# Down-projection between the gate/up groups of the next tile, and single buffers for row sums

## The chip, the cores and the metric

The kernel runs on one NeuronCore of a Trainium2 chip. The metric is the device time of one execution in microseconds (us). TensorE (PE) multiplies, with its weight loads shown apart (PEld); ScalarE (ACT) computes the exponentials and tanh; VectorE (DVE) adds, scales and moves results out of PSUM; GpSimd (POOL) does a few small steps; SyncE (SP) issues every DMA from one in-order queue.

## The reference

A pre-norm transformer block on x of 2048 tokens by 1024, all in bfloat16. Attention has 32 query heads of 32 columns, and one key and one value head for all of them. The second half is a gated feed-forward network with 3584 inner columns:

```
xn = layernorm(x)
q, k, v = xn @ wq, xn @ wk, xn @ wv          # 32 heads of q, one of k and of v
p = softmax(q @ k.T * 32 ** -0.5)            # per head, 2048 x 2048
h = x + (p @ v, heads side by side) @ wo
hn = layernorm(h)
out = h + (sigmoid(hn @ w_gate) * (hn @ w_up)) @ w_down
```

## The kernel before, in words

Tokens are cut into 16 tiles of 128. A tile's attention is four **blocks** (`qi`, 64 in all), each of 8 heads by 128 queries. A block is 8 **visits**: 8 score matmuls (`emit_S`, the rows with `S_ps<-QTb,kT`), then two exponentials on ACT of 128x1024 each (line 567). That makes 512 visits and 1024 exponentials. DVE adds the 8 results of a block up in `acc` (line 544, 14 adds), from which one short run of PE (`acc,sel`, 32 matmuls) makes the row sums; 64 matmuls with `Vt` then give the unscaled output of the block. Both are one group, `PV`. The reciprocals of the row sums go through DRAM and come back spread over the partitions (`r_scratch`, `rb`, lines 626 and 627), and DVE scales with them (line 630, `OT`). `acc`, `r_sb`, `rb` and `oun` each have two buffers, used in turn by blocks.

After a tile's four blocks come its output projection (`OP`, 16 matmuls of 512 columns with `wo_sb`), the second layernorm, its transposes (`hT`, line 714), and the feed-forward network. Its first part is 14 **gate/up groups** (`GU`, rows with `hnT,ring`, 32 matmuls of 128 columns each): seven column groups of 512, each a gate group and an up group. Each group reads one **weight slab** of 1 MB (1024 x 512), loaded from DRAM in four DMAs (line 744) into one of four slots of `ring`. The groups run forward in even and backward in odd tiles, so the last four slabs of a tile are the first four of the next, and a tile loads ten. A slab's slot is reloaded as soon as its group has run. Gate goes through tanh (line 781) and both make `hact` (line 787). The second part is the down-projection (`D`, rows with `zone,hact`): 56 matmuls of 512 columns in two groups of 28, whose weights stay in SBUF.

The order on each engine is written out before the kernel is built, by a planner in the kernel itself (`Plan`). It walks along PE's time with assumed costs; whenever the scores of the next visit can run and ACT's backlog is under 1 us it puts a visit, else it goes on with the current group, else it picks the first group that is ready by the list `PRIO` (line 365). A gate/up group is only taken when the plan has its slab landed, by an assumed 330 bytes per ns for all DMAs, and slab loads are spaced for 310 (lines 40 and 41): a load that the spacing holds back gets a wait on an ACT instruction. The engines then run these orders strictly, with semaphores.

Of the kernel before, what the change touches and what calls it, by code (L numbers as in the profile page):

```python
# [12 lines left out]
P = 128  # L13
# [22 lines left out]
class Plan:  # L36
# [3 lines left out]
    DMA_RATE = 330.0  # L40
    PACE_RATE = 310.0
# [99 lines left out]
def bass_sequential_preLN__grouped_kv_mqa__glu_gated_glu__prompt_kernel(  # L141
# [30 lines left out]
    with ExitStack() as es:  # L172
# [10 lines left out]
        acc = SB("acc", [2, 2048])  # L183
# [11 lines left out]
        hnT = SB("hnT", [2, DT, P])  # L195
        hact = SB("hact", [NFT * P])
# [10 lines left out]
        r_dram = nc.dram_tensor("r_scratch", [2, 16, 64], F32, kind="Internal").ap()  # L207
# [17 lines left out]
        qst = hact[:, :].rearrange("p (a b) -> p a b", b=512)  # L225
# [8 lines left out]
        extra = [acc[:, 0, :], hnT[:, :, :, :].rearrange("p a b c -> p (a b c)"), acc[:, 1, :],  # L234
                 hn[:, :, :].rearrange("p a b -> p (a b)")]
        acc_slots = (extra[0], extra[2])
# [128 lines left out]
        PRIO = ["xT", "KV", "Q0", "PV", "OP", "hT", "D", "GU", "Q1", "Q"]  # L365
# [17 lines left out]
        def mk_xT(t):  # L383
# [6 lines left out]
            def after(b, last):  # L390
                src = F_ps[:, b, :].bitcast(BF16).rearrange("p (a b) -> p a b", a=DT)
                fa, fd = both(xnT[:, :, t * P:(t + 1) * P], src)
                xT_ev[t] = evac(fa, fd, 1024, [last], 2, 1.92, bias=300.0)
                if t + 2 < NT:
                    make_norm1(t + 2, [last])
                    if (t + 2) % 4 == 3:
                        load_slab((t + 2) // 4, [xnorm[k] for k in range(t - 1, t + 3)])
                queue_after_xT(t)
                return [xT_ev[t]]
# [147 lines left out]
        acc_rel = []  # L547

        def emit_S(v):
# [14 lines left out]
            for i in range(2):  # L564
# [6 lines left out]
                if qi >= 2 and kp >= 1:  # L571
                    if acc_busy[0]:
                        late_adds.append((qi, kp, i))
                    else:
                        make_add(qi, kp, i)
# [10 lines left out]
        oun_ev = {}  # L586

        def mk_PV(qi):
            c, qd = qi // 4, qi % 4
            raw = qi < 2  # L590
            srcs = [slot_of[(qi, kp)] for kp in range(NKP)] if raw else [acc[:, qi % 2, :]]

            def sum_done(o):
                sum_last[qi] = o

# [24 lines left out]
            def after(b, last):  # L620
                k = qi % 2
                rc = pl.op("dve", lambda: DVE.reciprocal(r_sb[:, k, :], F_ps[:, b, 256:320]),  # L622
                           [last] + rb_ld.get(qi - 2, []), prio=0, occ=64 * 8 / 0.96 + 20, lat=64 * 8 / 0.96 + 90 + SEM)
                oc = pl.op("dve", lambda: DVE.tensor_copy(out=oun[:, k, :], in_=F_ps[:, b, 0:256]),  # L624
                           [last, ot_ev.get(qi - 2)], prio=0, **t_dve(256))
                r1 = dma(lambda: SP.dma_start(r_dram[k], r_sb[0:P:8, k, :]), f"rd{k}", 4096, [rc], prio=0)
                rb_ld[qi] = [dma(lambda: SP.dma_start(
                    rb[:, k, :], bass.AP(r_dram.tensor, r_dram.offset + k * 1024, [[256, 4], [0, DH], [1, 256]])),
                    f"rb{k}", 131072, [r1, ot_ev.get(qi - 2)], prio=0)]
                ot_ev[qi] = pl.op("dve", lambda: DVE.tensor_tensor(  # L630
                    out=OT[:, 2 * qd:2 * qd + 2, :], in0=oun[:, k, :].rearrange("p (a b) -> p a b", a=2),
                    in1=rb[:, k, :].rearrange("p (a b) -> p a b", a=2), op=ALU.mult),
                    [oc, op_last.get(c - 1)] + rb_ld[qi], prio=0, occ=330, lat=420)
# [16 lines left out]
        def release(qi, kp, o):  # L650
# [6 lines left out]
            else:  # L657
                extra_rel.append(o)
                if any(s is a for a in acc_slots):
                    acc_rel.append(o)  # L660
                    acc_busy[0] -= 1
                    if acc_busy[0] == 0:
                        for k in late_adds:
                            make_add(*k)
# [22 lines left out]
        def mk_OP(t, dc):  # L687
# [19 lines left out]
            def gate():  # L707
                return t in xr_ld and xr_ld[t].end is not None
            return Group("OP", atoms, lambda: [ot_ev[4 * t + i] for i in range(4)] + [wo_ld], after, gate)

        def mk_hT(t):
# [5 lines left out]
            def after(b, last):  # L717
                hT_last[t] = last
                src = F_ps[:, b, :].bitcast(BF16).rearrange("p (a b) -> p a b", a=DT)
                hT_ev[t] = pl.op("dve", lambda: DVE.tensor_copy(out=hnT[:, t % 2, :, :], in_=src),  # L720
                                 [last, gu_last.get(t - 2)] + (extra_rel if t < 2 else []), prio=1, **t_dve(1024, 1.92))
                for i in range(NGR):
                    mk_GU(t, i)
# [3 lines left out]


        def group_of(t, i):
            return i if t % 2 == 0 else NGR - 1 - i  # L730

        slab_seq = [(t, i, w) for t in range(NT) for i in range(NGR) for w in range(2) if t == 0 or i >= 2]
        slab_n = [0]
        slab_at = {}

        def load_slab(sl, deps):
            if slab_n[0] >= len(slab_seq):
                return
# [9 lines left out]
            slab_at[(t, i, w)] = (sl, ops)  # L748
            if i >= NGR - 2:
                slab_at[(t + 1, NGR - 1 - i, w)] = (sl, ops)  # L750

        hact_ev = {}
        n_gu = [0]
        box = {}

        def gu_deps(t):
            if t > 0:
                return [d_last[t - 1]]
            return q_store[-NQS:]

        def gu_gate(t, i, w):
# [247 lines left out]
```

## Time and profile before

| | |
|---|---|
| median of 2 runs | 1272.81 us (1267.83 to 1277.79) |
| profiled execution | 1273.21 us, span 1271.4 us |
| PE busy | 1137.9 us (89% of the span) |
| ACT busy | 1038.0 us (82%) |
| DVE busy | 849.2 us (67%) |
| DMA | 215 MB, mean 169 GB/s |

An engine's busy time is the sum of its instructions without overlaps. The profile names an instruction by its line, with output and input names (`F_ps<-hnT,ring` is a gate/up matmul); PE's line is that of a helper (L368), so one goes by the names. A wait is idle time of an engine and what ended it. Stretches are counted in us from the start of the span. The granted clock is a share of 2.4 GHz: 1.00 is 2.4 GHz, 0.50 is 1.2 GHz, and a value between is a mixture of both over the stretch.

### The profile page before, as it was taken

Reading aid. Unit: us, or ns where it says so; the run is one execution under the profiler, and the core shown is the slowest. Engines: PE = TensorE matmul, PEld = TensorE weight load, DVE = VectorE, ACT = ScalarE, POOL = GpSimd, SP = SyncE. Lnnn points to the kernel's source line nnn. Section 1 sums busy time; section 2 is a strip of 40 time slices with the busy share of each in tenths; the row PEclk is TensorE's granted clock in tenths of the full one; section 3 lists DMA queues with packets and bytes.
Section 4 is the critical chain, followed back from the end, with each engine's and each line's share of the span. In section 5 each row is a group of like instructions: output and inputs, shape, how many; then the busy total and the mean of one; then the engine's idle time right before and its main releaser. Section 6 shows DMA issues by size and latency. Waiting matters only on the chain.

```text
span 1271.4 us, 44591 instructions
## 1 busy us (share of the span) xinstructions
PE 1137.9 (89%) x19758; PEld 750.6 (59%) x19840; DVE 849.2 (67%) x1499; ACT 1038.0 (82%) x1154; POOL 54.6 (4%) x89
## 2 busy tenths in 40 slices
PE   5879969999999989998898999899998989989877
PEld 4644436565657565666566565656666564756554
DVE  8758867777767658676766768676767657666211
ACT  4769989899899889888999999889998978977000
POOL 3100000000000000000000000000000000000000
PEclk9989969999999999999999999999999999999999
DMA  9411397282829292747447191827446281734663
GB/s 309 142 30 52 100 330 237 81 274 93 258 69 296 64 293 84 234 132 226 152 134 234 54 320 34 267 86 226 154 159 210 65 280 33 235 120 156 196 221 128
DMA packets 218113, 215.11 MB, mean 169 GB/s; under 512 B 16832, under 2 KB 208320, under 8 KB 217920
## 3 DMA queue, kind: packets, MB, share of 16 engines
q1 hardware_dynamic: 217920, 212.26, 52.7%
q8 instruction: 155, 2.54, 0.8%
q14 instruction: 38, 0.31, 0.1%
HBM read 204.08 MB, written 8.13 MB: 167 GB/s over the span
## 4 chain that ended last, share of the span: by engine, by line
PE 54%; DMA 23%; ACT 12%; DVE 5%; issue 4%; SPq 2%; DVEq 0%
PE F_ps L368 45%; ACT Pr L567 11%; PE S_ps L368 8%; DMA ring<-in_B_w_gate_dram 8%; DMA r_scratch<-r_sb 5%; DMA ring<-in_B_w_up_dram 4%; DMA rb<-r_scratch 4%; DVE acc L544 1%; ACT tnh L781 1%; SPq L271 1%; DMA zone<-in_A_wq_dram 1%; DVE hact L787 1%; SPq L744 1%; DVE oun L624 0%; DVE st L315 0%
## 5 line engine op out<-in xcount | busy, mean ns | idle before, releaser
L567 ACT ACTIVATE Pr<-S_ps 128x1024 bf16<-128x1024 f32 x1016 | 970.8, 1030 | 103.2 <-PE S_ps L368 99.6
L544 DVE TENSOR_TENSOR acc<-acc,Pr 128x1024 bf16<-128x1024 bf16 x744 | 491.0, 686 | 113.0 <-ACT Pr L567 110.6
L368 PE MATMUL F_ps<-hnT,ring 128*128 128x128 bf16 x7168 | 481.9, 222 | 76.1 <-DMA ring<-in_B_w_gate_dram 38.9
L368 PEld LDWEIGHTS F_ps<-hnT,ring 128*128 128x128 bf16 x7168 | 413.3, 99 | 159.8 <-issue 68.0
L368 PE MATMUL S_ps<-QTb,kT 32*128 32x256 bf16 x4096 | 207.0, 277 | 13.3 <-ACT Pr L567 12.4
L368 PE MATMUL F_ps<-zone,hact 128*128 128x512 bf16 x841 | 204.2, 380 | 5.0 <-issue 3.1
L368 PE MATMUL F_ps<-Pr,Vt 128*32 128x256 bf16 x4064 | 141.1, 278 | 0.1
L781 ACT ACTIVATE tnh<-F_ps 128x512 f32<-128x512 f32 x112 | 67.1, 599 | 88.5 <-PE F_ps L368 82.3
L368 PEld LDWEIGHTS F_ps<-zone,hact 128*128 128x128 bf16 x896 | 78.9, 98 | 99.9 <-issue 20.5
L368 PEld LDWEIGHTS S_ps<-QTb,kT 32*128 32x128 bf16 x4096 | 61.1, 92 | 127.3 <-ACT Pr L567 73.7
L787 DVE SCALAR_TENSOR_TENSOR hact<-tnh,F_ps 128x512 bf16<-128x512 f32 x112 | 76.7, 685 | 87.9 <-PE F_ps L368 87.1
L544 DVE TENSOR_TENSOR acc<-Pr 128x1024 bf16<-128x1024 bf16 x124 | 84.1, 689 | 44.6 <-ACT Pr L567 43.7
L368 PEld LDWEIGHTS F_ps<-Pr,Vt 128*32 128x32 bf16 x4064 | 101.0, 98 | 19.7 <-issue 17.6
L630 DVE TENSOR_TENSOR OT<-oun,rb 128x256 bf16<-128x256 f32 x64 | 27.2, 425 | 88.9 <-DMA rb<-r_scratch 88.5
L368 PE MATMUL F_ps<-zone 128*128 128x512 bf16 (+3 forms) x566 | 74.1, 278 | 4.3 <-DVE zone L254 1.2
L368 PE MATMUL F_ps<-wo_sb,OT 128*128 128x512 bf16 x239 | 61.6, 390 | 5.8 <-ACT Pr L567 1.9
L326 POOL TENSOR_SCALAR zb<-mvb 128x1 bf16<-128x1 bf16 (+2 forms) x24 | 11.4, 476 | 1132.8 <-DVE mvb L322 1132.8
L368 PEld LDWEIGHTS F_ps<-zone 128*128 128x128 bf16 x576 | 40.0, 99 | 29.6 <-issue 8.2
L622 DVE RECIPROCAL r_sb<-F_ps 128x64 f32<-128x64 f32 x64 | 35.5, 555 | 25.0 <-PE F_ps L368 24.6
L819 DVE SCALAR_TENSOR_TENSOR h_sb<-F_ps,h_sb 128x512 bf16<-128x512 f32 x32 | 22.0, 689 | 30.6 <-PE F_ps L368 30.3
L368 PEld LDWEIGHTS F_ps<-wo_sb,OT 128*128 128x128 bf16 x256 | 21.9, 99 | 32.7 <-issue 9.2
L368 PEld LDWEIGHTS F_ps<-acc,sel 128*32 128x32 bf16 x2048 | 19.9, 98 | 20.0 <-issue 9.1
(57 smaller groups left out, 307.3 us busy)
## 6 DMA issues: line engine op xcount, KB each, us to landing
ring<-in_B_w_gate_dram SPq DMA_DIRECT2D x328, 256.0 KB, 4.6
ring<-in_B_w_up_dram SPq DMA_DIRECT2D x328, 256.0 KB, 4.8
rb<-r_scratch SPq DMA_DIRECT2D x64, 128.0 KB
zone<-in_B_w_down_dram SPq DMA_DIRECT2D x14, 512.0 KB, 7.0
ring<-in_A_x_dram SPq DMA_DIRECT2D x16, 256.0 KB, 6.0
h_sb<-in_A_x_dram SPq DMA_DIRECT2D x16, 256.0 KB, 3.8
out_dram<-h_sb SPq DMA_DIRECT2D x32, 128.0 KB, 1.8
QTb<-q_scratch SPq DMA_DIRECT2D x7, 512.0 KB, 5.8
```

The costliest lines, as they stand in the source:

```text
L271: x_ld[t] = dma(lambda: SP.dma_start(x_sb(t), xf[t * P:(t + 1) * P, :]), f"x{t}", P * D * 2, prio=0)
L326: f = pl.op("pool", lambda: POOL.tensor_scalar(out=zb[:, ph, tk], in0=mvb[:, ph, tk, 1], scalar1=LN_EPS_BF16, scalar2=None, op0=ALU.add), ...
L368: return lambda: PE.matmul(o, lhsT=l, rhs=r, start=start, stop=stop, **kw)
L544: add_op[(qi, kp, i)] = pl.op("dve", lambda: DVE.tensor_tensor(out=a, in0=in0, in1=slot[:, h], op=ALU.add), [exp_of[(qi, kp, i)]] + dp, pr ...
L567: exps[u] = pl.op("act", lambda i=i, pb=pb: ACT.activation(out=slot[:, i * 1024:(i + 1) * 1024].rearrange("p (a b) -> p a b", a=2), in_=S_ ...
L622: rc = pl.op("dve", lambda: DVE.reciprocal(r_sb[:, k, :], F_ps[:, b, 256:320]), [last] + rb_ld.get(qi - 2, []), prio=0, occ=64 * 8 / 0.96 ...
L630: ot_ev[qi] = pl.op("dve", lambda: DVE.tensor_tensor(out=OT[:, 2 * qd:2 * qd + 2, :], in0=oun[:, k, :].rearrange("p (a b) -> p a b", a=2), ...
L744: ops.append(dma(lambda q=q: SP.dma_start(wgu[:, sl, 2 * q:2 * q + 2, :], W[256 * q:256 * q + 256, gr * SW:(gr + 1) * SW].rearrange("(a p) ...
L781: box["a"] = pl.op("act", lambda: ACT.activation(out=tnh[:, :], in_=F_ps[:, b, :], func=ACTF.Tanh, scale=0.5), [last, box.get("e")], prio= ...
L787: e = pl.op("dve", lambda: DVE.scalar_tensor_tensor(out=hact[:, gr * 512:(gr + 1) * 512], in0=tnh[:, :], scalar=1.0, in1=F_ps[:, b, :], op ...
L819: e = pl.op("dve", lambda: DVE.scalar_tensor_tensor(out=h_sb[:, t % 4, sl], in0=F_ps[:, b, :], scalar=0.5, in1=h_sb[:, t % 4, sl], op0=ALU ...
```

## The change

The down-projection groups of a tile are no longer all placed ahead of the next tile's gate/up groups. A gate/up pass over the next tile starts first, and the two down groups fall due when 9 and 4 of its 14 groups are left (`d_due`, `PRIO_D`). So that both tiles' values can stand side by side, `hact` has room for two tiles, with the tiles interleaved by 128 columns, and the waits follow (`gu_deps`, `gu_gate`). The assumed DMA rates fall from 330 to 260 and from 310 to 250. To make room, `acc`, `r_sb`, `rb` and `oun` have one buffer each: the first add of a block waits for the row sums of the block before (`sum_last[qi - 1]`), and the reciprocal, its trip through DRAM and the copy to `oun` wait for those of the block before. The code can also run a pass over two tiles at once, with 256 columns; in the order as built this never happens: all 7168 gate/up matmuls still have 128 columns, and every engine has the same instructions in all, but for a few evacuations that change between ACT and DVE in the opening.

```diff
-    DMA_RATE = 330.0
-    PACE_RATE = 310.0
+    DMA_RATE = 260.0
+    PACE_RATE = 250.0
...
-        acc = SB("acc", [2, 2048])
+        acc = SB("acc", [2048])
...
-        r_sb = SB("r_sb", [2, 64], F32)
-        rb = SB("rb", [2, 256], F32)
+        r_sb = SB("r_sb", [64], F32)
+        rb = SB("rb", [256], F32)
...
-        oun = SB("oun", [2, 256], F32)
+        oun = SB("oun", [256], F32)
...
-        hact = SB("hact", [NFT * P])
+        hact = SB("hact", [NFT * 256])
...
-        PRIO = ["xT", "KV", "Q0", "PV", "OP", "hT", "D", "GU", "Q1", "Q"]
+        PRIO_D = ["xT", "KV", "Q0", "PV", "OP", "hT", "D", "GU", "Q1", "Q"]
+        PRIO = ["xT", "KV", "Q0", "PV", "OP", "hT", "GU", "D", "Q1", "Q"]
...
         def make_add(qi, kp, i):
+            if (not acc_rel) or (qi > 2 and (qi - 1) not in sum_last):
+                late_adds[qi].append((kp, i))
+                return
...
-                dp = [exp_of[(qi, 0, i)], sum_last.get(qi - 2)] + (acc_rel if qi < 4 else [])
+                dp = [exp_of[(qi, 0, i)]] + ([sum_last[qi - 1]] if qi > 2 else acc_rel)
...
-                rc = pl.op("dve", lambda: DVE.reciprocal(r_sb[:, k, :], F_ps[:, b, 256:320]),
-                           [last] + rb_ld.get(qi - 2, []), prio=0, occ=64 * 8 / 0.96 + 20, lat=64 * 8 / 0.96 + 90 + SEM)
+                rc = pl.op("dve", lambda: DVE.reciprocal(r_sb[:, :], F_ps[:, b, 256:320]),
+                           [last, rd_ld.get(qi - 1)], prio=0, occ=64 * 8 / 0.96 + 20, lat=64 * 8 / 0.96 + 90 + SEM)
...
+        def start_ffn():
+            t = ffn_next[0]
+            if queues["GU"] or t >= NT or t not in hT_ev or (t and (t - 1) not in gu_last):
+                return
+            if t + 1 in hT_ev:
+                ts = (t, t + 1)
+            elif t + 1 in hnorm and hnorm[t + 1].end is not None:
+                return
+            else:
+                ts = (t,)
...
+            nd = len(queues["D"])
+            for i in range(NGR):
+                for k in range(len(ts)):
+                    mk_GU(p, ts, i, k)
+            for k in range(nd):
+                d_due.append(len(queues["GU"]) * (nd - k) // (nd + 1))
...
-            if t > 0:
-                return [d_last[t - 1]]
-            return q_store[-NQS:]
+            return [d for t in ts for d in ([d_last[t - 2]] if t >= 2 else q_store[-NQS:] + extra_rel)]
...
-                    for cl in PRIO:
+                    pr = PRIO
+                    if d_due and len(queues["GU"]) <= d_due[0]:
+                        pr = PRIO_D
+                    for cl in pr:
```

What the planner makes of it, at three places. First PE where a tile's down groups (`zone,hact`) begin. Before: the last gate/up groups of a tile, and behind them its first down group.

```order
L368 MATMUL F_ps<-hnT,ring 128x128 x32
L368 MATMUL S_ps<-QTb,kT 128x256 x8
L368 MATMUL F_ps<-hnT,ring 128x128 x24
L368 MATMUL F_ps<-zone,hact 128x512 x2
L368 MATMUL S_ps<-QTb,kT 128x256 x8
L368 MATMUL F_ps<-zone,hact 128x512 x7
L368 MATMUL S_ps<-QTb,kT 128x256 x8
L368 MATMUL F_ps<-zone,hact 128x512 x7
L368 MATMUL S_ps<-QTb,kT 128x256 x8
L368 MATMUL F_ps<-zone,hact 128x512 x12
```

And PE now, at the first down group of a tile:

```order
L368 MATMUL F_ps<-hnT,ring 128x128 x15
L368 MATMUL F_ps<-zone,hact 128x512 x5
L368 MATMUL S_ps<-QTb,kT 128x256 x8
L368 MATMUL F_ps<-zone,hact 128x512 x8
L368 MATMUL S_ps<-QTb,kT 128x256 x8
L368 MATMUL F_ps<-zone,hact 128x512 x7
L368 MATMUL S_ps<-QTb,kT 128x256 x8
L368 MATMUL F_ps<-zone,hact 128x512 x6
L368 MATMUL S_ps<-QTb,kT 128x256 x8
L368 MATMUL F_ps<-zone,hact 128x512 x2
L368 MATMUL F_ps<-acc,sel 32x64 x32
```

Down matmuls came once a tile's 14 groups were through; now 28 of them stand behind the fifth group of the next tile and 28 behind the tenth.

Second DVE where one block ends and the next begins (`acc<-Pr` are the two adds that begin a block, the reciprocal belongs to the block before). Before:

```order
L544 TENSOR_TENSOR acc<-Pr 128x1024 [waits s_act] x2
L544 TENSOR_TENSOR acc<-acc,Pr 128x1024 [waits s_dve,s_act] x3
L819 SCALAR_TENSOR_TENSOR h_sb<-F_ps,h_sb 128x512 [waits s_pe]
L544 TENSOR_TENSOR acc<-acc,Pr 128x1024 [waits s_dve,s_act] x2
L622 RECIPROCAL r_sb<-F_ps 128x64 [waits s_pe]
L624 COPY oun<-F_ps 128x256
```

And now:

```order
L854 SCALAR_TENSOR_TENSOR h_sb<-F_ps,h_sb 128x512 [waits s_pe]
L548 TENSOR_TENSOR acc<-Pr 128x1024 [waits s_pe,s_act]
L548 TENSOR_TENSOR acc<-Pr 128x1024 [waits s_act]
L548 TENSOR_TENSOR acc<-acc,Pr 128x1024 [waits s_dve,s_act] x2
L626 RECIPROCAL r_sb<-F_ps 128x64 [waits d_rd,s_pe]
L628 COPY oun<-F_ps 128x256
```

The first add of a block waited for ACT alone and now for PE too; before the reciprocal of the block before stand four adds in place of seven.

Third PE behind the last visit. Before:

```order
L368 MATMUL F_ps<-hnT,ring 128x128 x82
L368 MATMUL F_ps<-acc,sel 32x64 x32
L368 MATMUL F_ps<-Pr,Vt 32x256 x64
L368 MATMUL F_ps<-hnT,ring 128x128 x128
L368 MATMUL F_ps<-wo_sb,OT 128x512 x16
L368 MATMUL F_ps<-hnT,ring 128x128 x96
L714 MATMUL F_ps<-ident,hn 128x128 x8
L368 MATMUL F_ps<-hnT,ring 128x128 x32
L368 MATMUL F_ps<-zone,hact 128x512 x56
L368 MATMUL F_ps<-hnT,ring 128x128 x448
L368 MATMUL F_ps<-zone,hact 128x512 x56
```

And now (nine down matmuls and 32 of a gate/up group stand before these rows):

```order
L368 MATMUL F_ps<-acc,sel 32x64 x32
L368 MATMUL F_ps<-Pr,Vt 32x256 x64
L368 MATMUL F_ps<-hnT,ring 128x128 x128
L368 MATMUL F_ps<-zone,hact 128x512 x28
L368 MATMUL F_ps<-wo_sb,OT 128x512 x16
L368 MATMUL F_ps<-hnT,ring 128x128 x128
L715 MATMUL F_ps<-ident,hn 128x128 x8
L368 MATMUL F_ps<-zone,hact 128x512 x28
L368 MATMUL F_ps<-hnT,ring 128x128 x320
L368 MATMUL F_ps<-zone,hact 128x512 x28
L368 MATMUL F_ps<-hnT,ring 128x128 x128
L368 MATMUL F_ps<-zone,hact 128x512 x56
```

Before, 786 gate/up and 112 down matmuls are left there; now 736 and 149, and the longest unbroken gate/up run falls from 448 to 320.

## Rows read from the trace of the kernel before

**Rows 1.** Busy time by stretch: us, each engine (instructions), granted clock, DMA share, GB/s.
```profile
200.00:1166.00 966.00, 893.85 (x15896) 594.47 (x15956) 680.46 (x1169) 871.67 (x963) 33.80 (x42) 0.99 0.53 168
1166.00:1272.00 106.00, 82.71 (x995) 60.16 (x996) 19.55 (x33) 8.27 (x14) 1.35 (x3) 0.97 0.60 193
```
**Rows 2.** Waits from 200 to 1166 us: waiting for whom, total us, times, longest.
```profile
DVE acc L544 <- ACT Pr L567: 141.9, 254, 2.6
...
DVE OT L630 <- DMA rb<-r_scratch: 78.6, 50, 4.5
...
PEld F_ps L368 <- DMA ring<-in_B_w_gate_dram: 41.3, 52, 3.3
...
PEld F_ps L368 <- DMA ring<-in_B_w_up_dram: 18.8, 26, 2.3
...
PEld F_ps L368 <- DVE acc L544: 5.7, 22, 0.4
```
**Rows 3.** Groups of the page's part 5: exponentials and tanh on ACT.
```profile
L567 ACT ACTIVATE Pr<-S_ps 128x1024 bf16<-128x1024 f32 x1016 | 970.8, 1030 | 103.2 <-PE S_ps L368 99.6
...
L781 ACT ACTIVATE tnh<-F_ps 128x512 f32<-128x512 f32 x112 | 67.1, 599 | 88.5 <-PE F_ps L368 82.3
```
**Rows 4.** Busy time by stretch: six tile periods; the first, the longest, their sum.
```profile
706.76:775.52 68.76, 65.19 (x1164) 42.92 (x1170) 50.00 (x86) 64.23 (x72) 2.62 (x3) 1.00 0.56 178
...
989.33:1066.33 77.00, 67.72 (x1165) 44.96 (x1170) 50.17 (x86) 64.51 (x72) 2.62 (x3) 0.96 0.50 152
...
sum 432.90, PE 395.59 PEld 261.14 DVE 300.69 ACT 386.30 POOL 15.74; mean PE 65.93 PEld 43.52 DVE 50.12 ACT 64.38 POOL 2.62
```
**Rows 5.** Waits for slabs in those six periods (706.76 to 1139.66 us).
```profile
PEld F_ps L368 <- DMA ring<-in_B_w_gate_dram: 28.4, 37, 3.3
...
PEld F_ps L368 <- DMA ring<-in_B_w_up_dram: 9.8, 16, 2.3
```
**Rows 6.** Timeline of a tile: start, us, engine, instruction, count [idle before <- releaser].
```profile
643.54 1.68 PE L368 MATMUL F_ps<-zone,hact 128*128 128x512 bf16 x7
...
648.61 0.69 DVE L544 TENSOR_TENSOR acc<-Pr 128x1024 bf16<-128x1024 bf16 x1 [1.53 <-ACT Pr L567]
...
649.38 0.42 PE L368 MATMUL F_ps<-acc,sel 128*32 128x64 bf16 x32
...
649.62 1.39 PE L368 MATMUL F_ps<-Pr,Vt 128*32 128x256 bf16 x44
...
653.20 1.96 PE L368 MATMUL F_ps<-hnT,ring 128*128 128x128 bf16 x32
...
655.09 0.40 PE L368 MATMUL S_ps<-QTb,kT 32*128 32x256 bf16 x8
```
**Rows 7.** Timeline of PE in 1040 to 1045 us, behind slab waits.
```profile
1040.92 2.42 PE L368 MATMUL F_ps<-hnT,ring 128*128 128x128 bf16 x23
```
**Rows 8.** Busy time by stretch: the same 5 us.
```profile
1040.00:1045.00 5.00, 4.57 (x90) 3.48 (x94) 1.72 (x3) 3.04 (x5) 0.00 (x0) 0.66 0.90 284
```
**Rows 9.** DMA issues by line: KB each, median us from issue to landing.
```profile
ring<-in_B_w_gate_dram SPq DMA_DIRECT2D x328, 256.0 KB, 4.6
```
**Rows 10.** Waits from 1166 us to the end.
```profile
PEld F_ps L368 <- DMA ring<-in_B_w_up_dram: 15.7, 23, 1.9
...
PEld F_ps L368 <- DMA ring<-in_B_w_gate_dram: 10.3, 16, 1.5
```
**Rows 11.** Timeline of PE from the last visit to the end.
```profile
1164.44 0.40 PE L368 MATMUL S_ps<-QTb,kT 32*128 32x256 bf16 x8
...
1201.26 12.03 PE L368 MATMUL F_ps<-zone,hact 128*128 128x512 bf16 x54
1213.13 7.53 PE L368 MATMUL F_ps<-hnT,ring 128*128 128x128 bf16 x132
...
1256.43 12.03 PE L368 MATMUL F_ps<-zone,hact 128*128 128x512 bf16 x54
```

More of the change, by code (lines that the diff above doesn't have):

```diff
@@ L590, in mk_PV @@
             raw = qi < 2
-            srcs = [slot_of[(qi, kp)] for kp in range(NKP)] if raw else [acc[:, qi % 2, :]]
+            srcs = [slot_of[(qi, kp)] for kp in range(NKP)] if raw else [acc[:, :]]
             def sum_done(o):
                 sum_last[qi] = o
+                if qi >= 2:
+                    flush_adds(qi + 1)
             def atoms(b):
@@ L707, in gate @@
             def gate():
-                return t in xr_ld and xr_ld[t].end is not None
+                return t in xr_ld and xr_ld[t].end is not None and (t < 2 or (t - 2) in hT_last)
             return Group("OP", atoms, lambda: [ot_ev[4 * t + i] for i in range(4)] + [wo_ld], after, gate)
@@ L761, in gu_gate, with gu_deps, mk_GU, shape @@
-        def gu_gate(t, i, w):
-            return (t, i, w) in slab_at and (q_left[0] == 0 if t == 0 else d_done[t - 1] == 2)
-        def mk_GU(t, i):
-            gr = group_of(t, i)
+        def gu_deps(ts):
+            return [d for t in ts for d in ([d_last[t - 2]] if t >= 2 else q_store[-NQS:] + extra_rel)]
+        def gu_gate(p, ts, i, w):
+            return (p, i, w) in slab_at and all(q_left[0] == 0 if t < 2 else d_done[t - 2] == 2 for t in ts)
+        def mk_GU(p, ts, i, k):
+            gr = group_of(p, i)
+            n = P * len(ts)
+            fs = range(4) if len(ts) == 1 else range(2 * k, 2 * k + 2)
+            f0 = 4 * gr + fs[0]
+            hs = hact[:, :].rearrange("p (f a b) -> p f a b", a=2, b=P)[:, f0:f0 + len(fs)]
+            if len(ts) == 1:
+                ho = hs[:, :, ts[0] % 2, :]
+                mv_h = hnT[:, :, ts[0] % 2, :]
+            else:
+                ho = hs
+                mv_h = hnT[:, :, :, :].rearrange("p d a b -> p d (a b)")
+            def shape(ap):
+                if len(ts) == 1:
+                    return ap.rearrange("p (f b) -> p f b", b=P)
+                return ap.rearrange("p (f a b) -> p f a b", a=2, b=P)
@@ L787, in after_u @@
                 e = pl.op("dve", lambda: DVE.scalar_tensor_tensor(
-                    out=hact[:, gr * 512:(gr + 1) * 512], in0=tnh[:, :], scalar=1.0, in1=F_ps[:, b, :],
-                    op0=ALU.add, op1=ALU.mult), [last, box["a"]] + gu_deps(t), prio=0, **t_dve(512))
+                    out=ho, in0=shape(tnh[:, :]), scalar=1.0, in1=shape(F_ps[:, b, :]),
+                    op0=ALU.add, op1=ALU.mult), [last, box["a"]] + gu_deps(ts), prio=0, **t_dve(512))
                 box["e"] = e
-                for f in range(4):
-                    hact_ev[4 * gr + f] = e
+                for t in ts:
+                    for f in fs:
+                        hact_ev[(t, 4 * gr + f)] = e
@@ L805, in mk_D @@
-        def mk_D(t, dc):
-            ev = dict(hact_ev)
-            order = [4 * group_of(t, i) + f for i in range(NGR) for f in range(4)]
+                if i == NGR - 1 and fs[-1] == 3:
+                    for t in ts:
+                        gu_last[t] = last
+                        for dc in range(2):
+                            queues["D"].append(mk_D(p, t, dc))
+                return [e]
+            queues["GU"].append(Group("GU", atoms(0), lambda: [hT_ev[t] for t in ts] + slab_at[(p, i, 0)][1][0:1], after_g,
+                                      lambda: gu_gate(p, ts, i, 0)))
@@ L826, in after @@
                 return [e]
-            return Group("D", atoms, lambda: [ev[ft] for ft in order[:-8]] + [wd_ld[order[0]]], after)
+            return Group("D", atoms, lambda: [hact_ev[(t, ft)] for ft in order[:-8]] + [wd_ld[order[0]]], after)
         for t in range(NT):
```

122 lines of the change are left out of this document (57 added, 65 removed).

## The prediction, made before the changed kernel was run

> **What bounds the kernel now.** I read busy time by stretch first. Between 200 and 1166 us PE is busy for 894 of 966 us and ACT for 872 [rows 1]: neither is full, so something makes both wait. That stretch holds 15896 matmuls at 1164 to a tile, 13.66 tiles or 54.6 blocks, and so 70.7 us to a tile. ACT alone would need less: 970.8 us over 1016 exponentials is 0.956 us each, 64 of them and 7 tanh of 0.60 us make 65.3 us [rows 3]. PE's waits show what is missing. Its weight loads wait 41.3 + 18.8 = 60.1 us for slabs, in 78 waits of up to 3.3 us [rows 2]. PE runs its list strictly, so while it waits for a slab no scores come either, and with PE and ACT both over nine tenths full the loss is not caught up. Six tile periods bear that out: they take 432.9 us, 72.15 each [rows 4], and contain 38.2 us of slab waits [rows 5]; without them a tile would take 65.8, half a microsecond above ACT's 65.3. So the middle is bound by ACT and PE together, and **slab waits lie on the path** one for one.
>
> Why slabs are late: 32 gate/up matmuls and the visit behind them take 2.2 us [rows 6], so a running gate/up phase eats a slab every 2.2 us. The load side is seen at the end, where 448 gate/up matmuls run with nothing between: 43.3 us from 1213.13 to 1256.43 [rows 11]. The first four slabs were there, 7.2 us of work; the ten others came in 36.1 us, 3.6 us each. Through 14 groups in a row the lead of four slabs melts; then, in the down groups, the ring is full and the DMAs rest.
>
> A long wait also costs clock. Behind slab waits near 1040 us the granted clock is 0.66 over 5 us, a mixture of 2.4 and 1.2 GHz [rows 8], and 23 gate/up matmuls take 2.42 us [rows 7], 105 ns each against 1.96 / 32 = 61 [rows 6]. Over the middle the mean clock is 0.99 [rows 1], some 10 us of withheld clock.
>
> **The change, part by part.** The instructions are the same ones; the two-tile pass is never built, so not one slab load is saved. All that moves is order, and who waits for whom.
>
> *Down groups between gate/up groups.* A tile now runs 5 groups, 28 down matmuls, 5 groups, 28 down matmuls, 4 groups. Twenty-eight down matmuls with their four visits take 28 x 1.68/7 + 4 x 0.33 = 8 us [rows 6], so five slabs get 11 + 8 = 19 us, about the 18 us that they take at 3.6, and ten get a whole tile of 66 us. The lower assumed rate holds loads back to 1.05 MB / 250 = 4.2 us a slab, 42 us for ten: still inside 66. What stays is the start of a run: the first slot is free after 2.2 us, its four pieces go out over 3.1 us and the last needs 4.6 us to land [rows 9], 9.9 us in all, while the fifth group wants it after 8.9. That is 1 us once a tile, or 14 us if nothing covers it; a row-sum group of about 2 us often will. Bounds: nothing gained (0) and every slab wait gone (-60). I take 85% of them, **-51 us**, because of that 1 us.
>
> *Clock.* Bounds 0 and -10; not every dip follows a slab wait. **-5 us**.
>
> *Single `acc`.* Today the first add of a block starts at 648.61, before the row sums of the block before, which run from 649.38 to 649.80 [rows 6]. Now it must wait for them: 1.2 us later here, and DVE's list behind it too. The cover is DVE's slack: it waits 141.9 us in the middle for exponentials [rows 2], 2.6 us a block, and PE waits for DVE's last add in 22 places for 5.7 us in all [rows 2]. The add chain is late by 1.2 and has 2.6 to catch up in, so I charge half of that 5.7 again, **+3 us**; if the cover were gone it would be the second rival.
>
> The general rule speaks against this step: the Trainium skill, page "Trainium Kernel Development and Optimization", section Best Practices, says to double-buffer so that transfer and compute overlap. By the rule every block would pay for its lost buffer, and the sum would lose the 1.2 us in 54.6 blocks, 66 us, all the gain; by the row the slack of 2.6 us takes it in, and the row decides here.
>
> *Single `r_sb`, `rb`, `oun`.* The reciprocal of a block waits for a trip that began a whole block, 16.5 us, earlier. DVE's waits for `rb` are 78.6 us in 50 places, 4.5 at most [rows 2], well short of 16.5. Nothing, bounds 0 and +3. The interleaved `hact` costs nothing that I can see: the same elements from the same PSUM bank; bounds 0 and +1.
>
> *SP's queue.* Row-sum trips stand in the one queue with the slab loads and are moved past some. A load held back for spacing delays the trip behind it by up to 4.2 us. It is covered as long as DVE does not reach the scaling step first; I put it into the second rival.
>
> *The end.* From the last visit (1164.44 + 0.4) to 1271.4 it takes 106.6 us, with 26.0 us of slab waits [rows 10]. More work is left there now: 37 down matmuls more at 11.87 / 56 = 0.212 us [rows 11], 50 gate/up fewer at 7.53 / 132 = 0.057, so +5. In the new order: 9 down 1.9, 32 gate/up 1.8, row sums and `Vt` 2.3 [rows 6], 128 gate/up 7.3, 28 down 5.9, 16 output projection 3.4, 128 gate/up 7.3, transposes 0.5, 28 down 5.9, together 36.3. Then the last tile: 320 gate/up, 28 down, 128 gate/up. Its ten loads still come at 3.6 us each, so I give it the 43.3 us of before, but the 28 down matmuls now lie inside. Then 15.0 as before from 1256.43. That is 94.6, 12 less; 2 of it I leave for a slab wait in the first part. **-10 us**; bounds +5 (no wait saved) and -21 (all 26 saved).
>
> The Trainium skill, page "DMA: Bandwidth & Descriptors", section Specifications, gives about 358 GB/s from memory for one core; a slab would then take 2.9 us, and the end would be some 7 us shorter again, 1203 in all. The row shows 3.6, and I go by it.
>
> *Opening* (to 200 us): the same work in nearly the same order, 0, bounds -5 and +5.
>
> **Sum**: -51 - 5 + 3 - 10 = -63, against the profiled execution's 1273.2 us (span 1271.4 and 1.8 around it; the median of the runs is 1272.8, the same): **1210 us**. The middle would take 66.8 us a tile, above ACT's 65.3.
>
> **Rivals.**
>
> *The slabs stay late.* The new spacing holds loads back although the DMAs could go faster, and if a slab takes 4.2 us and more, each of the three runs in a tile begins with a wait. For it: the 1 us computed above, with landing times that have been 4.6. Against: the DMAs are busy 53% of the middle [rows 1], and ten slabs have 66 us. With half of the waits left: -30 - 2 + 3 - 5 = -34, so 1239.
>
> *The add chain becomes the bound*, the single `acc` outweighing all else. Row sums are taken only right behind a visit, so they can be a visit of 1.9 us later than in the row above: the first add is then 1.2 + 1.9 = 3.1 us later than today, and a slower `rb` takes from the same slack, 78.6 / 50 = 1.6 us where it waits [rows 2]. DVE's busy time is 50.1 of 72.15 us a tile [rows 4], so in a tile of 66 each block leaves 4.0 us for all its waits. What exceeds the slack of 2.6 makes the last add late, PE stands at the row sums, and the scores behind it. Each microsecond of that costs 54.6 us. It decides at 66 / 54.6 = 1.2 us a block: there the gain of 66 us (without the +3) is gone. With 1.0 us it is 1262; with the full 3.1 + 1.6 - 2.6 = 2.1 us it is 1273 - 66 + 115 = 1322, slower. For it: four adds in place of seven fit before the reciprocal. Against: the longest wait of PE for an add is 0.4 us [rows 2], and other DVE work can fill the gap.
>
> **How the numbers follow.** Forecast 62%, late slabs 17%, the add chain 19% (12% about even, 7% slower), something else 2%. A difference of under 2%, about 25 us, can't be told from no change. The forecast lies below 1247, and so does most of late slabs: faster 75%. The rest of that and the even part of the chain: same 18%. Slower 7%. The forecast's own range is 1185 (the middle at ACT's 65.3 us, -74, and -14 at the end) to 1232; with late slabs and the beginning of the chain case the range is 1185 to 1255.
>
> **What would show it.** Waits for `ring` between 200 us and the last visit: under 15 us for me, 30 for the first rival. Waits of PE for `acc`: under 10 us for me, over 50 for the second. The tile period: 66 to 67.5 us for me. The end behind the last visit: 92 to 99 us. DMA slices more even than now. I am wrong if PE's waits for slabs stay, if PE waits for DVE at the row sums, or if tiles stay above 69 us with neither, which would mean that the plan's new order has holes of its own.

## The result and the profile after

The changed kernel takes **1190.57 us** (1190.39 to 1190.74, 2 runs) against 1272.81: ratio 0.935, 95% interval 0.920 to 0.951. Run once more on one chip with 15 runs of the kernel before (median 1268.56) it is 1193.8 us, ratio 0.943 (0.939 to 0.947). The forecast was 1210, the range 1185 to 1255.

The page's second part shows the loads first. Its rows for the DMAs, in 40 slices, of the kernel before:

```profile
DMA  9411397282829292747447191827446281734663
GB/s 309 142 30 52 100 330 237 81 274 93 258 69 296 64 293 84 234 132 226 152 134 234 54 320 34 267 86 226 154 159 210 65 280 33 235 120 156 196 221 128
```

And of the changed kernel:

```profile
DMA  9512187565666666565737483746628383747583
GB/s 307 171 33 59 50 295 229 186 198 175 198 194 189 201 191 207 149 217 179 236 115 238 120 255 119 240 150 208 203 89 247 120 252 89 232 147 213 166 267 106
```

Up to the middle of the execution the swing between full and idle, 9 and 2, is gone, and behind it is smaller. The bytes are the same.

Busy time by stretch of the changed kernel (us, then each engine with its instructions, granted clock, DMA share, GB/s); its last visit starts at 1090.62, where it was 1164.44 [rows 11]:

```profile
0.00:200.00 200.00, 163.22 (x2905) 95.28 (x2905) 152.57 (x304) 160.68 (x182) 20.04 (x44) 0.94 0.51 160
200.00:1091.00 891.00, 872.67 (x15939) 585.66 (x15932) 659.93 (x1163) 864.52 (x959) 32.91 (x42) 1.00 0.60 185
1091.00:1188.00 97.00, 84.71 (x1009) 60.81 (x1005) 20.32 (x35) 8.68 (x14) 1.34 (x3) 0.98 0.60 188
```

PE is now busy for 98% of the middle and ACT for 97; before it was 93 and 90 [rows 1]. From the first to the last row sums behind 200 us, 54 blocks or 13.5 tiles in both traces, it is 892.4 us (202.41 to 1094.78) against 962.1 (209.58 to 1171.72): **66.1 us a tile against 71.3** (the prediction's 70.7 was counted by matmul records, over another stretch).

Waits in the middle of the changed kernel, 200 to 1091 us (for whom, total us, times, longest):

```profile
DVE acc L548 <- ACT Pr L573: 41.6, 93, 4.2
DVE OT L634 <- DMA rb<-r_scratch: 39.3, 40, 2.7
...
DVE acc L548 <- PE F_ps L368: 28.1, 18, 2.9
...
PE F_ps L368 <- DVE h_sb L854: 5.0, 5, 1.5
...
PEld F_ps L368 <- DVE acc L548: 3.0, 9, 0.8
...
PEld F_ps L368 <- DMA ring<-in_B_w_up_dram: 2.3, 3, 1.4
PEld F_ps L368 <- DMA ring<-in_B_w_gate_dram: 1.9, 2, 1.5
```

They answer to [rows 2]. Slab waits are down from 60.1 to 4.2 us. DVE waits for PE at the first add of a block, 28.1 us that did not exist before: that is the single `acc`. DVE waits 100 us less for exponentials, and PE's wait for its last add did not grow (3.0 against 5.7). The cost has gone into DVE's slack.

PE's timeline behind the last visit (start, us, engine, instruction, count, idle before and its releaser), beside [rows 11]:

```profile
1090.62 0.40 PE L368 MATMUL S_ps<-QTb,kT 32*128 32x256 bf16 x8
1090.95 2.12 PE L368 MATMUL F_ps<-zone,hact 128*128 128x512 bf16 x9
1092.90 1.95 PE L368 MATMUL F_ps<-hnT,ring 128*128 128x128 bf16 x32
...
1096.89 7.32 PE L368 MATMUL F_ps<-hnT,ring 128*128 128x128 bf16 x128
1104.04 6.21 PE L368 MATMUL F_ps<-zone,hact 128*128 128x512 bf16 x28
1110.09 3.62 PE L368 MATMUL F_ps<-wo_sb,OT 128*128 128x512 bf16 x16
1113.54 7.31 PE L368 MATMUL F_ps<-hnT,ring 128*128 128x128 bf16 x128
...
1127.69 7.53 PE L368 MATMUL F_ps<-hnT,ring 128*128 128x128 bf16 x132
1135.43 0.28 PE L368 MATMUL F_ps<-hnT,ring 128*128 128x128 bf16 x2 [0.21 <-DMA ring<-in_B_w_gate_dram]
...
1151.15 1.85 PE L368 MATMUL F_ps<-hnT,ring 128*128 128x128 bf16 x30 [1.35 <-DMA ring<-in_B_w_gate_dram]
...
1155.56 6.21 PE L368 MATMUL F_ps<-zone,hact 128*128 128x512 bf16 x28
...
1169.84 0.28 PE L368 MATMUL F_ps<-hnT,ring 128*128 128x128 bf16 x2 [1.04 <-DMA ring<-in_B_w_up_dram]
...
1173.12 12.72 PE L368 MATMUL F_ps<-zone,hact 128*128 128x512 bf16 x56
```

The end takes 98.2 us (1188.8 - 1090.6) against 107.0. The pieces ahead of the last tile come as summed; from 1135 on, in the last tile, PE waits for slabs again.

### The profile page after: what moved, and what is told of

Its sections match the earlier page's. It is cut to its first block, busy times and chain, and to the rows that moved or that the text cites. A ratio compares the mean times of both kernels' runs of the same rounds, so it can differ in the third digit from the quotient of the medians.

```text
span 1188.8 us, 44836 instructions
## 1 busy us (share of the span) xinstructions
PE 1120.6 (94%) x19840; PEld 741.8 (62%) x19840; DVE 832.8 (70%) x1500; ACT 1033.9 (87%) x1153; POOL 54.3 (5%) x89
## 4 chain that ended last, share of the span: by engine, by line
PE 72%; DMA 8%; ACT 8%; DVE 7%; issue 3%; SPq 1%; DVEq 0%
PE F_ps L368 61%; PE S_ps L368 11%; ACT Pr L573 7%; DMA rb<-r_scratch 4%; DVE acc L548 2%; DMA r_scratch<-r_sb 2%; DMA ring<-in_B_w_gate_dram 1%; DMA ring<-in_B_w_up_dram 1%; SPq L764 1%; DVE st L312 1%; DVE st L314 1%; DVE zone L253 1%; ACT tnh L814 1%; DVE ring L344 1%; DVE zone L351 0%
## 5 line engine op out<-in xcount | busy, mean ns | idle before, releaser
L548 DVE TENSOR_TENSOR acc<-acc,Pr 128x1024 bf16<-128x1024 bf16 x744 | 480.9, 683 | 39.2 <-ACT Pr L573 38.0
L368 PE MATMUL F_ps<-hnT,ring 128*128 128x128 bf16 x7168 | 458.6, 220 | 20.6 <-DMA ring<-in_B_w_up_dram 7.2
L368 PEld LDWEIGHTS F_ps<-hnT,ring 128*128 128x128 bf16 x7168 | 405.4, 98 | 88.1 <-issue 64.4
L368 PE MATMUL F_ps<-zone,hact 128*128 128x512 bf16 x896 | 216.0, 381 | 0.8 <-DVE oun L628 0.5
L548 DVE TENSOR_TENSOR acc<-Pr 128x1024 bf16<-128x1024 bf16 x124 | 80.7, 686 | 45.5 <-PE F_ps L368 30.2
L368 PE MATMUL F_ps<-wo_sb,OT 128*128 128x512 bf16 x256 | 65.1, 385 | 2.4 <-ACT Pr L573 1.2
L695 DVE TENSOR_TENSOR h_sb<-F_ps,h_sb 128x512 bf16<-128x512 f32 x32 | 22.0, 689 | 25.8 <-PE F_ps L368 25.4
```

The lines of the kernel that those rows point to most:

```text
L368: return lambda: PE.matmul(o, lhsT=l, rhs=r, start=start, stop=stop, **kw)
L548: add_op[(qi, kp, i)] = pl.op("dve", lambda: DVE.tensor_tensor(out=a, in0=in0, in1=slot[:, h], op=ALU.add), [exp_of[(qi, kp, i)]] + dp, pr ...
L695: h_ev[(t, dc)] = pl.op("dve", lambda: DVE.tensor_tensor(out=h_sb[:, t % 4, sl], in0=F_ps[:, b, :], in1=h_sb[:, t % 4, sl], op=ALU.add), [ ...
```

## The experiments

To follow them it helps to see PE's list for one settled tile of each plan. G is a gate/up group (32 matmuls, one slab), D a down group (28), O the output projection, v the row sums with `Vt`, and a dot is one visit of 8 score matmuls. The changed plan differs somewhat from tile to tile; the tile shown begins at 675 us:

```
before     G.G.G.G.G.G.G..v.G.G.G.G...v.O..G.G.G.D....v..D....v.
changed    G..GG..v.G.G.D.....vG.G..G.G.O...vG.D.....G..vG..G.G.
e2         G.G.G.G.G..vG.G..GG..O...vG.G..G..G.G.v.D....D.....v.
e4, e8     G..vG.G.G.G..GO..v..G.G.G.G..v.G.G.G...G..D...v.D....
e7         G.G.G.G.O..v..G.G.G.G.G..v.G.G.G.G.G...v.D....D....v.
e10        G.G.G..vG.G..GG..O...vG..G.G..G.G..v.D....D....v.G.G.
```

What they gave (slab waits are those of PE's weight loads from 200 us to the last visit; the end is from the last visit to the span's end; middles are alike only where the end holds the same work):

| run | us | ratio to before | slab waits | end |
|---|---|---|---|---|
| before | 1272.8 | 1 | 60.1 | 107.0 |
| changed | 1190.6 | 0.935 (0.920-0.951) | 4.2 | 98.2 |
| e1 before, half slabs | 1196.2 | 0.942 (0.937-0.948) | 19.8 | 93.4 |
| e2 single buffers only | 1236.7 | 0.976 (0.970-0.981) | 36.1 | 98.7 |
| e3 interleaved, old rates | 1249.6 | 0.985 (0.979-0.991) | 33.1 | 99.1 |
| e4 low rates only | 1317.6 | 1.039 (1.033-1.045) | 71.1 | 182.6 |
| e5 changed again | 1193.8 | 0.943 (0.939-0.947) | 5.1 | 95.9 |
| e6 last slabs early | 1179.9 | 0.932 (0.928-0.936) | 2.4 | 85.4 |
| e7 before at 310/290 | 1253.1 | 0.989 (0.986-0.993) | 36.1 | 127.8 |
| e8 single buffers, low rates | 1315.7 | 1.039 (1.034-1.044) | 71.9 | 182.9 |
| e9 spacing alone low | 1209.2 | 0.952 (0.948-0.956) | 18.3 | 99.1 |
| e10 down groups side by side | 1232.1 | 0.972 (0.965-0.978) | 35.5 | 121.5 |
| e11 before at 325/305 | 1244.4 | 0.980 (0.975-0.985) | 38.2 | 108.8 |
| e12 changed, half slabs | 1171.2 | 0.924 (0.920-0.928) | 1.3 | 89.1 |

**Are slab waits on the path? (e1, e12)** Both load only half of each slab's columns; the other half of the weights is left out. The order is untouched.

```diff
-                    wgu[:, sl, 2 * q:2 * q + 2, :],
-                    W[256 * q:256 * q + 256, gr * SW:(gr + 1) * SW]...
+                    wgu[:, sl, 2 * q:2 * q + 2, 0:SW // 2],
+                    W[256 * q:256 * q + 256, gr * SW:gr * SW + SW // 2]...
```

> The kernel before with its order untouched, but each slab DMA fetches only the first 256 of its 512 columns (the other half of the slot keeps old data, so the output is another one). Theory (slab waits lie on the path one for one): the 60 us of slab waits in the middle and most of the 26 us at the end go, and 5 to 10 us of clock come back: 1180 to 1195 us. Rival (PE and ACT meet another wait once slabs are early): most of it stays, 1230 us or more.

> The changed kernel with every slab DMA fetching only 256 of its 512 columns (the other half of the weights is left out), order and spacing as they are. It shows what slabs still cost: the 13.0 us of waits at the end and 4.2 in the middle should nearly go, 1175 to 1182. If the middle went on waiting for slabs in ways that the list of waits doesn't show, such as slower DMA trips for the row sums, it would fall further, to 1165 or less.

Waits of e1 in its middle:

```profile
PEld F_ps L368 <- DMA ring<-in_B_w_gate_dram: 14.6, 16, 1.9
PEld F_ps L368 <- DMA ring<-in_B_w_up_dram: 5.2, 10, 1.6
```

With the order of before and half the bytes the time is 1196.2, 73 us below the 1269.5 beside it, and 52.5 us of slab waits have gone (40.3 in the middle, 12.2 at the end). It is 1 us above the range of the theory, and 34 below the rival's. So late slabs held the kernel before. The 20 us beyond the 52.5 are not shown to be theirs: with half the bytes DVE's waits for `rb` fall too, from 78.6 to 29.1 us, and the mean granted clock rises from 0.974 to 0.984. In the changed kernel the same cut gives 1171.2, 4 below the forecast of this run: the middle, too, got 0.8 us a tile shorter (881.8 us over 13.5 tiles, 65.3 each), where only 3 us of slab waits were to be had. The trips of `rb` landed earlier: DVE's waits for them fall from 39.3 to

```profile
DVE OT L634 <- DMA rb<-r_scratch: 12.1, 19, 2.6
```

and PE's waits for `h_sb` from 5.0 to 1.1. Whether these two make up the rest was not tried apart. That 65.3 is also the figure that the prediction had for ACT's own time is chance. Busy time of e12 over the 54 blocks (PE, PEld, DVE, ACT and POOL in turn):

```profile
202.57:1084.40 881.83, 863.58 (x15865) 586.55 (x15933) 660.72 (x1162) 862.59 (x958) 32.42 (x41) 1.00 0.36 104
```

ACT is busy for 862.6 us there, 63.9 a tile (64.4 in the kernel before [rows 4]). The prediction's 65.3 is an average over the whole execution and no floor. At 66.1 ACT is 97% busy, so little is left below it all the same.

**Which part of the change does it? (e2, e3, e4, e8)** e2 and e8 undo the interleaving, e2 and e3 the low rates; e4 is the kernel before with the low rates alone. The edits, in the changed kernel:

```diff
-                    pr = PRIO                                   # e2, e8
-                    if d_due and len(queues["GU"]) <= d_due[0]:
-                        pr = PRIO_D
+                    pr = PRIO_D
...
-    DMA_RATE = 260.0                                            # e2, e3
-    PACE_RATE = 250.0
+    DMA_RATE = 330.0
+    PACE_RATE = 310.0
...
-            if t + 1 in hT_ev:                                  # e8
-                ts = (t, t + 1)
-            elif t + 1 in hnorm and hnorm[t + 1].end is not None:
-                return
-            else:
-                ts = (t,)
+            ts = (t,)
```

> The changed kernel with the down groups ahead of the gate/up groups again and the assumed rates of before (330 and 310): single buffers are nearly all that is left of the change. Theory: the slack of DVE covers the lost buffers, at most +3 us on before, 1268 to 1278 us. Rival (the add chain becomes the bound, as the double-buffer rule has it): 1300 us or more, with PE waiting for acc over 50 us.

> The changed kernel with the assumed rates of before (330 and 310): interleaving and single buffers alone. In its order only 637 gate/up and 112 down matmuls are left behind the last visit, against 736 and 149. Theory A (interleaving spreads the loads, the rates only trim): slab waits in the middle under 15 us, and the shorter end makes it as fast as the change or faster, 1178 to 1195 us. Theory B (the lower rates are what keeps PE from running into its slabs): slab waits of 30 us or more return, 1205 to 1235 us.

> The kernel before with nothing but the assumed rates of the change (260 and 250). In its order 1344 gate/up and 183 down matmuls are left behind the last visit: three tiles of the feed-forward network. Theory A (interleaving does it): the middle runs at ACT's pace without slab waits, but the end then needs some 30 slab loads at 3.6 us with little beside them, 140 to 150 us from the last visit, 1225 to 1245 us in all. Theory B (the rates do it): 1185 to 1205 us.

> The changed kernel with the down-projection ahead of gate/up again (and the two-tile pass switched off), rates 260 and 250. PE's list is the same as in e4 but for single groups here and there, and as many groups are left behind the last visit (1344 gate/up, 183 down); what differs is single buffers for acc, r_sb, rb and oun, and room for two tiles in hact. If single buffers cost nothing: the time of e4, 1317.6, within 10 us. If each block pays 1.2 us for its one acc: 1360 or more. If the single buffers were what made e2 fast: 1290 or less.

Slab waits in the middle of e3, and then of e4:

```profile
PEld F_ps L368 <- DMA ring<-in_B_w_up_dram: 18.5, 32, 1.8
...
PEld F_ps L368 <- DMA ring<-in_B_w_gate_dram: 14.6, 27, 1.6
```

```profile
PEld F_ps L368 <- DMA ring<-in_B_w_up_dram: 35.6, 51, 2.0
PEld F_ps L368 <- DMA ring<-in_B_w_gate_dram: 35.5, 37, 3.2
```

No part is the change. The new priorities at the old rates (e3) give 20 us; slab waits came back as its theory B had it, but the time is 15 us above that theory's range. The low rates alone (e4) cost 48: the plan then takes gate/up groups later, three tiles of the network (1344 gate/up matmuls instead of 786) are left behind the last visit, and the end grows to 182.6 us. Against the expectation its middle kept its slab waits, more of them than before. Why is not settled. It may be that slabs spaced at 4.2 us, longer than the 3.6 that a slab needs [rows 11], are overtaken sooner where no down group stands between the gate/up groups; no run tries that by itself. Holding loads back is not enough to make them late: SyncE waits for ACT before slab loads for 189.9 us in the middle of e4 and for 204.5 in that of the changed kernel. Together the two give 75 us (1268.6 to 1193.8 in e5, on the same chip).

Single buffers alone were expected to be neutral or to cost; e2 gained 33. The pair e4 and e8 shows that buffers are not what gained: two lists of PE that are nearly the same, with double and with single buffers, end at 1317.6 and 1315.7, ratio 1.039 both. Sixty-four blocks at 1.2 us would have been 77 us. **The single buffers cost nothing there.** A tile of that pair takes some 69 us, so DVE has more slack in it than in a tile of 66; no run has the changed order with double buffers, and for the changed kernel itself the evidence is PE's 3.0 us of waits for `acc`. What e2 has is another plan: five groups ahead of the first row sums instead of seven.

**Does it matter where a plan happens to cut? (e7, e11)** Both are the kernel before with nothing but its two constants shifted.

```diff
-    DMA_RATE = 330.0
-    PACE_RATE = 310.0
+    DMA_RATE = 310.0      # e11: 325.0
+    PACE_RATE = 290.0     # e11: 305.0
```

> The kernel before with its two assumed rates at 310 and 290 in place of 330 and 310, nothing else: all buffers double, down-projection ahead of gate/up. In this plan the output projection and the row sums fall behind the fourth, ninth and fourteenth gate/up group of every tile instead of behind the eighth and twelfth. Theory (what counts is only how many gate/up groups follow one another without other PE work, whatever cuts them): slab waits in the middle fall from 60 to under 15, the last visit comes at 1090 to 1105 us; 896 gate/up and 148 down matmuls are left behind it, more than in the kernel before, and take 110 to 120 us: 1200 to 1225. Rival (it takes the down-projection between the groups, or the far lower rates): the middle keeps 40 us or more of slab waits, and the time is 1250 or more.

> The kernel before with its two assumed rates at 325 and 305 in place of 330 and 310, nothing else; all buffers stay double. In this plan a tile's gate/up groups follow one another as in e2: five, row sums, and the rest in smaller pieces, where the kernel before has seven at first. 843 gate/up matmuls are left behind the last visit (764 in e2), which is 5 us of PE work more. If e2 owed its 33 us to where its plan happened to put the cuts, and not to its single buffers: slab waits in the middle of 30 to 45 us and a time of 1230 to 1255. If the single buffers did it: 1262 to 1280, with slab waits near 60.

e11, with all buffers double and a list like that of e2, has 38.2 us of slab waits and 1244.4: as the theory of cuts said, so that the plan explains most of e2's gain (26 us here on its chip against 33, with 5 us more work at the end). e7 failed my expectation: the time is the rival's, 1250 or more. Its runs of groups are cut after 4, 9 and 14 by the output projection and row sums, and 36.1 us of waits stay, where under 15 were expected. Its 14 groups pass in 19 visits, some 39 us at 66 / 32 a visit, and then two down groups stand side by side while the ring is full. Row sums and projection, 2 and 3.4 us, seem too short to let the loads catch up; that is argued and not tried apart.

**Is it the place of the down groups, or the low rates? (e9, e10)** e9 raises the assumed landing rate alone; e10 keeps all and moves only the two due times.

```diff
-    DMA_RATE = 260.0                                                             # e9
+    DMA_RATE = 330.0
...
-                d_due.append(len(queues["GU"]) * (nd - k) // (nd + 1))           # e10
+                d_due.append(2)
```

> The changed kernel with the assumed landing rate back at 330 and only the spacing of loads left at 250; this splits the two constants that e3 undid together. As much work is left behind the last visit as in the changed kernel. If the spacing is what keeps the plan's gate/up groups apart: under 10 us of slab waits in the middle, 1188 to 1205. If the plan needs the low landing rate, as it then takes groups whose slab isn't there: 30 us or more of slab waits as in e3, 1225 to 1250.

> The changed kernel with the same buffers and rates; only the two due times differ: both down groups fall due when 2 of 14 gate/up groups are left, so they stand side by side behind the 13th, and the gate/up groups follow one another as in the kernel before. 907 gate/up and 168 down matmuls are left behind the last visit instead of 736 and 149. Theory (the gain is that down groups part the gate/up groups, so that no run of them outpaces its loads): slab waits come back in the middle, 1.5 to 5 us a tile, 20 to 60 in all; the end is 14 us of PE work longer and waits more for slabs there; 1225 to 1265. Rival (the low rates do it wherever the down groups stand): the middle stays under 10 us of slab waits with its last visit near 1090, and only the end grows, to 112 to 120 us: 1203 to 1212.

Slab waits in the middle of e10:

```profile
PEld F_ps L368 <- DMA ring<-in_B_w_up_dram: 24.5, 40, 1.7
...
PEld F_ps L368 <- DMA ring<-in_B_w_gate_dram: 11.0, 16, 2.0
```

Same rates, same buffers, the down groups side by side: 35.5 us of slab waits come back, and the gain shrinks from 75 us to 40 (1272.3 beside e10 to 1232.1). Its middle is 18 us longer than that of the changed kernel, although some 14 us of PE's work have moved from there to the end, which is 23 us longer: 32 us in the middle for 31 us more of slab waits. The rival, that low rates suffice wherever the down groups stand, falls. e9 lies between both expectations: 18.3 us of waits, 1209.2. So the spacing is the larger half of what e3 lacked (1249.6 to 1209.2), and the assumed landing rate gives the rest (to 1193.8).

**The rest of the end (e5, e6).** e6 fetches the last tile's six middle slabs into slots of `Pr` that are free behind the last block.

```diff
+                if qi == NQ - 1:
+                    for k in range(6):
+                        load_slab(NSLAB + k, [last], NT - 1, 2 + k // 2, k % 2, prio=5)
```

> The changed kernel as it is, once more on the same chip as the three runs beside it, for a narrower interval. 1190 again (1185 to 1196): in the first trace its middle runs at 65.3 us a tile, ACT's own time, and 98 us follow the last visit. Above 1210 would mean that the plan's gain depends on the execution.

> The changed kernel, but the six middle slabs of the last tile are fetched into Pr slots that are free once the last block is done, so that the last tile does not wait for its ring. If the 13.0 us of slab waits behind the last visit lie on the path one for one, they shrink to 2 or 3 and the time falls by 8 to 12 us, to 1178 to 1183. Rival: the last tile is bound by how fast DMAs bring ten slabs (36 us at 3.6), wherever they land, or PE's other work there hides it; then 1187 to 1192. The middle should not move: last visit at 1090 to 1092 us.

(The 65.3 us a tile that the first of these gives for the changed kernel is 66.1 by its row sums.)

PE's timeline at the end of e6:

```profile
1152.92 5.75 PE L370 MATMUL F_ps<-hnT,ring 128*128 128x128 bf16 x100
1159.69 0.29 PE L370 MATMUL F_ps<-hnT,ring 128*128 128x128 bf16 x2 [1.02 <-DMA ring<-in_B_w_up_dram]
1160.31 1.63 PE L370 MATMUL F_ps<-hnT,ring 128*128 128x128 bf16 x26 [0.33 <-DMA ring<-in_B_w_up_dram]
1161.77 12.25 PE L370 MATMUL F_ps<-zone,hact 128*128 128x512 bf16 x56
```

Slab waits at the end fall from 10.9 us (e5) to 1.7, and the time from 1193.8 to **1179.9 us** on the same chip, ratio to before 0.932 (0.928 to 0.936): the fastest full version here. The drop of 14 is 2 more than the theory had, with the last visit unmoved (1091.86 against 1092.87). The wait was on the path, and memory could bring the slabs in time.

Part of that wait seems to come from the one queue of SyncE. Its issues in the last tile of the changed kernel:

```profile
1157.24 1.72 SPq L764 DMA_DIRECT2D ring<-in_B_w_gate_dram  x3
1162.52 0.36 SPq L857 DMA_DIRECT2D out_dram<-h_sb  x1
1162.92 0.44 SPq L764 DMA_DIRECT2D ring<-in_B_w_gate_dram  x1
1164.26 2.79 SPq L764 DMA_DIRECT2D ring<-in_B_w_up_dram  x4
```

Between three quarters of a slab and its last quarter stands an output store that must wait for the down-projection. The queue stands still behind it until 1162.5, and PE waits for the slab after that one between 1167 and 1171. In e6 the same store stands before three pieces of the last slab. This is read from the traces; no run moved the store.

## Why the prediction was right, and where its sizes were off

The mechanism is the one forecast: down groups between gate/up groups let the loads keep up, and the middle goes to 66.1 us a tile (forecast 66 to 67.5). By its terms, against the profiled executions (82.6 us between the spans; the middle is from 200 us to the last visit):

- *Slab waits in the middle, -51*: as forecast. The waits of PE's weight loads fell by 56, 60.1 to 4.2. PE itself stood idle for slabs only 41 us less (44.8 to 3.4, by the rows of its gate/up matmuls in the middle, before and then changed):

```profile
L368 PE MATMUL F_ps<-hnT,ring 128*128 128x128 bf16 x6190 | 413.2, 221 | 55.8 <-DMA ring<-in_B_w_gate_dram 31.3 <-DMA ring<-in_B_w_up_dram 13.5 <-DVE mv L317 5.3
```

```profile
L368 PE MATMUL F_ps<-hnT,ring 128*128 128x128 bf16 x6239 | 398.0, 219 | 10.2 <-DVE h_sb L854 5.0 <-DMA ring<-in_B_w_up_dram 1.8 <-DMA ring<-in_B_w_gate_dram 1.6
```

  The rest of each wait is hidden in PE's busy time. One matmul's record lasts 0.22 us in both kernels (221 and 219 ns), but in a run the next one begins after 0.061, so the records overlap. At a stop the last record stands alone, and some 0.16 us of it count as busy although PE takes no new work:

```profile
882.27 0.28 PE L368 MATMUL F_ps<-hnT,ring 128*128 128x128 bf16 x2 [0.43 <-DMA ring<-in_B_w_gate_dram]
882.98 0.23 PE L368 MATMUL F_ps<-hnT,ring 128*128 128x128 bf16 x1 [0.43 <-DMA ring<-in_B_w_gate_dram]
```

  There are 60 such stops for slabs in the middle of the kernel before and 4 in the changed one: an estimate of 10 us, and with the 41 it is 51. The cause is sound: half the bytes in the old order (e1), and the old neighbourhood with everything else new (e10), show it from both sides.
- *Clock, -5, bounds 0 and -10*: **mis-sized**, it came near its outer bound. PE's busy time in the middle fell by 20 us, 892 to 872, for nearly the same work; the gate/up matmuls have 18 of it (66.7 ns each against 63.8, over 6200). 10 us are the stops above. The rest, some 10 us, fits the granted clock: some 24 us of the old middle ran at 1.2 GHz (a granted clock of 0.50), which costs 12 us at most, and none of the new one.
- *Other waits, not listed*: **put at nothing without a reason**. PE's idle time by other causes fell as well, 27 to 15 us (72.2 and 18.3 in all, less 44.8 and 3.4 for slabs). Some 4 of these 12 stand as idle time that waits for nothing, and the trace of the kernel before lacks 82 of PE's 19840 matmul records, so they may be no waits at all. One of the others I should have seen: a down group right behind its tile's last gate/up group waited for `hact`, 4.4 us in 5 places; five groups later it is long there, 0.4. New is a wait of 5.0 us for `h_sb`.
- *Single `acc`, +3*: nothing. It did delay the first add (28.1 us of DVE waits in 18 places), and DVE's 2.6 us of slack a block took it in. The row decided against the Trainium skill's rule of double buffers (page "Trainium Kernel Development and Optimization", section Best Practices), and e8 beside e4 shows the same, where 66 us would be plain to see. The page says it of DMA and compute. `acc` lies between two engines; `rb`, which a DMA fills, is nearer to the rule, and the waits for it fell too (next point).
- *Single `r_sb`, `rb`, `oun`, 0*: DVE's waits for `rb` fell from 78.6 to 39.3.
- *The end, -10*: 107.0 to 98.2, -9; its slab waits went from 26.0 to 13.0, and the added work and the `Vt` pieces came as summed.
- *Opening, 0*: three visits more lie before 200 us (82 against 79), some 6 us.

So the middle was forecast at -53 and came at -74 (964.4 to 890.6 us): some -51 of slab waits, -10 of clock, -12 of other idle time and nothing for `acc`, where I had -51, -5, 0 and +3. 6 us of the -74 are the opening's three visits. What was off by some 20 us is thus the clock, the idle time that I did not list and `acc`; the price of a slab wait, one for one, was right. The time came 5.6 us above the lower end of the range, which stood on a middle at ACT's 65.3 us and an end at -14; e6, at 1179.9, shows that this was no floor. Both rivals fell: PE waits 3.0 us for `acc`, not 50, and slabs at a spacing of 4.2 us are late in e10, not in the changed kernel.

## What to carry to other kernels

A stream of loads that is fast enough on average still stalls its reader if the reader takes it in runs: put the work that needs no loads between pieces of the run, long enough for the loads to catch up (pieces of 6 us did it here, with loads spaced; pieces of 2 to 3.4 us only in part), and test the order and its spacing constants as a pair, since either alone may lose. A second buffer is worth only the part of the wait it saves that exceeds the waiting engine's slack: read that engine's waits before paying for one. A plan that comes out of assumed costs is touchy: shifting two constants by under 2% moved this kernel by 2%, so a gain of one part alone (e2) may belong to the plan's cuts and not to the part.

## What the hardware showed that was not expected

A busy PE hides part of each stop: a lone gate/up matmul between two waits shows 0.23 us of busy time, where one in a run takes up 0.061. So PE's idle time alone (44.8 us) understates what late slabs cost; the waits of its weight loads (60.1) do not.

And loads that are spaced land sooner. The median from issue to landing of a slab's quarter is 4.0 us in the changed kernel and 4.6 before [rows 9], with the same bytes in less time:

```profile
ring<-in_B_w_gate_dram SPq DMA_DIRECT2D x328, 256.0 KB, 4.0
```

It goes with the spacing, and hardly with the order. By the same row of the other runs it is 4.7 us at 310 bytes per ns (e2, e3), 4.5 at 305 (e11), 4.3 at 290 (e7), and 3.7 to 4.1 at 250 (e4, e5, e8, e9, e10). e3 has the new order at the old rates, e4 the old order at the new ones.
